# One-core recurrent attention with two MLP layers: keys of weight pieces renamed in a planned instruction order, one x split listed earlier, due times set anew

## The chip, the cores and the metric

The kernel runs on one core of one Trainium2 chip. The metric is device time in microseconds (us) of one execution, as the median of several runs. The engines are TensorE (PE in the profile; PEld is its load of the stationary operand), VectorE (DVE), ScalarE (ACT), GpSimd (POOL) and SyncE (SP, which issues the DMA transfers of this kernel). Each engine works through its own list of instructions in order.

## The reference

```python
def _attn_ref(r, k, v, w, u):          # B, H, S, D = 4, 8, 768, 48
    state = zeros(B, H, D, D)
    for t in range(S):
        cur = einsum('bhd,bhe->bhde', u[None] * k_t, v_t)
        y[:, :, t] = einsum('bhd,bhde->bhe', r_t, state + cur)
        state = w_t[:, :, :, None] * state + einsum('bhd,bhe->bhde', k_t, v_t)
x = attention output as 3072 tokens of 384
h = maximum(maximum(x @ w1, x @ w2), x @ w3)   # 384 -> 768
x = h @ w_out                                  # 768 -> 384
h = x @ w_in                                   # 384 -> 1024
solu = h * softmax(h)
out = (layernorm(solu) * g_ln) @ w_out         # 1024 -> 384
```

All of it is float32. The weights arrive as 64-bit words.

## The kernel before

**Units.** The sequence is cut into chunks of 128 tokens: 6 chunks of 4 batches give 24 units, numbered chunk by chunk, so that units 0 to 3 are the first chunk of the four batches and unit u takes the state that unit u - 4 left. `attend(u)` lists the steps of one unit: SP loads w, k, r (the feature-major parts, `load_part`), rk (token-major r and k) and v. DVE runs two scans over w, `s_sfx` (sf, L399, with pts L404 and a reciprocal) and `s_pfx` (pf, L416), scales r (rp, L420), multiplies rk by u and reduces it (rku, L433 and L439), and masks the scores (L481). POOL scales k (kt, L402), multiplies r by k (L429) and builds the diagonal (L449). TensorE computes the scores (sc, L474), up to unit 4 transposes k (kTp, L651), and then y in two parts: intra (L536) and, behind the state matmuls ds (L582), inter (L548). DVE ends the state (sbd, L610); from unit 5 on DVE also transposes k (kq, L632) for a trip through DRAM. ACT copies y out as xf (L662) and SP gathers rows of it (L668).

**Tiles.** Units form the tiles of the MLP: tile 0 is units 0 and 1, tile 1 is units 2 and 3, tile 2 is units 4 and 5; the later six tiles have three units each. `split(u)` turns x of unit u into a high part xh (ACT, L688) and a low part xl (POOL, L687), since each product is made of three matmuls. `layer_a(j)` lists 18 groups a{j}_{f}_{m} of nine matmuls (L737), six f by three m (w1, w2, w3). The first of the three results is copied by ACT (L742), the other two are folded in by DVE with max (L744); ACT and POOL then split h (L747, L750). `layer_b(j)` is the second matrix (L767). The groups a and b, the transposes and the conversion of weights share four PSUM banks.

**Weights.** The first layer's weights come in 24 pieces. `convert` lists for each: a load by SP (L1036), three ACT instructions (L311 to L313), a pair on DVE (L318, L323), then the high part (ACT, L332) and the low part (POOL, L336). Piece i, for i below 18, is what group i = 3f + m of a layer reads. Four raw buffers serve the loads, seven from piece 13 on, which lie over buffers of units 1 to 3.

**The order.** Nothing here is ordered by hand. `P.add` (L110 on) gives the planner a task: engine, estimated time, due time, and keys that it reads and writes. Dependencies come from the keys in the order in which tasks are listed: a reader depends on the last writer of the key, a writer on the last writer and all readers since. `order` then fills the engines in its own estimated time, and of the tasks that can start takes the one due first. Only the resulting lists reach the chip; there the engines wait for real buffers and results alone, not for the planner's keys. So a dependency between two things that merely share a key is a constraint on the order, and not a wait on the chip.

```python
r_, k_, w_ = ("r", u % 2), ("k", u if u < 3 else (u - 3) % 2), ("w", u if u < 3 else (u - 3) % 2)
add("SP", 400, -9000, lambda: load_part(u, 2), writes=[w_], kb=260)
done = convert(conv, "c", "w", C_DUE[0], C_DUE[1], 1.0, 384, banks=True, ...)
[(x_, k) for k in range(n)] + [("w", i)]
```

The first two lines are the keys of a unit's buffers in `attend`, with ("w", 0) to ("w", 2) for w; the third gives the converted pieces the keys ("w", 0) to ("w", 23); the fourth is what a group of `layer_a` reads. `due_of(u)` derives a unit's due times from `START`; `C_DUE` is the due time of the first piece and the step between pieces; `START[0]` and `START[1]` are those of layer a of tiles 0 and 1.

Of the kernel before, what the change touches and what calls it, by code (L numbers as in the profile page):

```python
# [23 lines left out]
KF1 = FF1 // 128  # L24
# [13 lines left out]
POST = (0, 1, 2, 2)  # L38
C3 = (4, 9, 1, 1, 1)
GAIN = 1  # L40
START = (34000, 48000, 100000, 7000)
BOTH, STEP, AHEAD = 41000, 45600, 20000
C_DUE = (14000, 3000)
SLACK = 1500
CUT = 0.5
GRP = [(0, 0), (0, 0), (0, 0), (1, 1), (1, 1, 1, 2)]
# [131 lines left out]
def emit(tc, general, flag, fm, tm, ub, wa, win, wo2, g, cst, half_cst, lmask, out):  # L178
# [9 lines left out]
    with ExitStack() as top:  # L188
# [481 lines left out]
        def s_xt(u):  # L670
            if u not in xf:
                return
            j = tile_of[u]
            n = tiles[j] * L
            if j not in xt:
                if j == 1:
                    o = 2 * KF1 * n
                    xt[j] = tuple(flat(wi)[:, o + i * KX * n:o + (i + 1) * KX * n].rearrange("p (a b) -> p a b", a=KX)
                                  for i in range(2))
                else:  # L680
                    if general or "x" not in xt:
                        xt["x"] = [xpool.tile([128, KX, n_max], F32R, tag=f"x{a}", name=f"x{a}{j}") for a in "hl"]
                    xt[j] = [t[:, :, 0:n] for t in xt["x"]]
            o = (u - first[j]) * L
            xh, xl = xt[j]
            x = xf.pop(u)
            low = lambda: G.tensor_tensor(xl[:, :, o:o + L], x[:, 0:KX], xh[:, :, o:o + L].bitcast(F32), op=ALU.subtract)  # L687
            A.activation(xh[:, :, o:o + L], x[:, 0:KX], AF.Copy)  # L688
            if general:
                low()  # L690
            else:
                at[u]["xl"] = low
# [109 lines left out]
        def second_weights():  # L802

            if not general:
# [22 lines left out]
        conv = Conv([sl(2 * (N_TMP + i), 2) for i in range(N_RAW)], [[sl(2 * t + i) for i in range(2)] for t in range(N_TMP)], jobs,  # L827
                    [stage[:, SPARE + 2 * i * CW:SPARE + 2 * (i + 1) * CW] for i in range(3)], SWITCH)
# [138 lines left out]
        def fast_phase1():  # L967
            P = Plan({"m": 4, "s": 1, "y": 1})
            n_unit = lambda j: range(first[j], first[j] + tiles[j])
            need = [START[0], START[1], START[2]]  # L970
            for j in range(3, n_tile):
                need.append(need[-1] + (BOTH if j == 3 else STEP))

            def due_of(u):
                j = tile_of[u]
                last = need[j] - AHEAD
                gap = (need[j] - need[j - 1]) / tiles[j] if j > 1 else START[3]
                return last - gap * (first[j] + tiles[j] - 1 - u)
# [47 lines left out]
            def split(u, after=()):  # L1026
                x_, o_ = ("xf", u % 3), (("x1" if tile_of[u] == 1 else "x"), u - first[tile_of[u]])
                P.add("ACT", 510, due_of(u) + 13000, lambda: s_xt(u), [x_], [o_], after)
                P.add("POOL", 1100, due_of(u) + 14000, lambda: at[u]["xl"](), [], [x_, o_])

            def convert(c, name, out, due, step, size, kb, after=(), extra=None, banks=False):
                lows = []
                for i in range(len(c.jobs)):
                    raw, tmp = (name, "raw", c.slot[i]), (name, "tmp", i % len(c.tmps))
                    t = due + step * i
                    P.add("SP", 400, t - 9000, lambda i=i: nc.sync.dma_start(c.raws[i], c.jobs[i][0]), [],  # L1036
                          [raw] + (extra(i) if extra else []), after, kb=kb)
                    key = ("m", (name, i)) if banks else None
                    bank = lambda: ps_m.tile([128, CW], F32, tag="m", name="cv") if banks else None
                    P.add("ACT", 1700 * size, t - 4000, lambda i=i: c.stage0(i, bank()), [raw], [tmp], take=key)  # L1040
                    P.add("DVE", 1150 * size, t - 2500, lambda i=i: (c.stage1(i), c.stage2(i)), [raw], [tmp], give=key,
                          port=0 if banks else 700)
                    P.add("ACT", 520 * size, t - 1200, lambda i=i: c.high(i), [tmp], [(out, i)])
                    P.add("POOL", 1100 * size, t - 1000, lambda i=i: c.low(i), [], [tmp, (out, i)])
                    lows.append(P.tasks[-1])
                return lows
# [3 lines left out]
            def layer_a(j, due, step, after=()):  # L1050
                n = tiles[j]
                sa, sb_, cur = moe[j] = moe_groups(j)
                x_, h_ = ("x1", "h1") if j == 1 else ("x", "h")
                for f in range(KF1):
                    for m in range(3):
                        key = ("a", j, f, m)
                        t_ = ("t", j, f % KX if j > 1 else 0)
                        i = 3 * f + m
                        g_ = P.add("PE", 9 * (174 if n == 3 else 120), due + step * i, lambda f=f, m=m: sa(f, m),
                                   [(x_, k) for k in range(n)] + [("w", i)], [("order", j)], take=("m", key))  # L1060
                        P.add("DVE" if m else "ACT", 560 if n == 3 else 430, 0, lambda f=f, m=m: cur["up", f, m](),
                              [], [t_], [g_, *after], give=("m", key))
                    P.add("ACT", 540 if n == 3 else 430, 0, lambda f=f: cur["hh", f](), [t_], [(h_, f)])
                    P.add("POOL", 1080 if n == 3 else 850, 0, lambda f=f: cur["hl", f](), [], [t_, (h_, f)])

            def layer_b(j, due, step, after=()):
                n = tiles[j]
                sa, sb_, cur = moe[j]
                h_ = "h1" if j == 1 else "h"
                w = 174 if n == 3 else 120  # L1070
                out = []
                for f0, f1 in ((0, KF1 - 1), (KF1 - 1, KF1)):
                    for m in range(KX):
                        key = ("b", j, m)
                        g_ = P.add("PE", 3 * (f1 - f0) * w, due + step * len(out), lambda m=m, f0=f0, f1=f1: sb_(m, f0, f1),
                                   [(h_, f) for f in range(f0, f1)] + [("w", 3 * KF1 + f) for f in range(f0, f1)] + [("order", j)],
                                   [("b", m)],
                                   take=("m", key) if f0 == 0 else None)
                        out.append(g_)
                for m in range(KX):  # L1080
                    P.add("ACT", 500 if n == 3 else 380, 0, lambda m=m: cur["x2", m](), [("b", m)], [], after,
                          give=("m", ("b", j, m)))
                return out
# [2 lines left out]
            P.add("SP", 400, 6000, lambda: nc.sync.dma_start(ident, cst[:, 128:]), [], ["ident"], kb=64)  # L1086
            P.add("SP", 400, 5000, lambda: nc.sync.dma_start(cs, half_cst), [], ["cs"], kb=64)
            for u in range(B):
                attend(u)
            over_spare = [[("k", 2), ("w", 2)], [("k", 2), ("w", 2), ("a", True)], [("a", True), ("rk", 2)]]  # L1090
            done = convert(conv, "c", "w", C_DUE[0], C_DUE[1], 1.0, 384, banks=True,
                           extra=lambda i: over_spare[conv.slot[i] - N_RAW] if conv.slot[i] >= N_RAW else [])
            for u in n_unit(0):
                split(u)
            layer_a(0, START[0], 2200, after=[])
            for u in n_unit(1):
                split(u)
            layer_a(1, START[1], 2200)
            for u in n_unit(2):
                attend(u)  # L1100
            for u in n_unit(2):
                split(u)
            b0 = layer_b(0, need[2] - 3000, 1500, done)
            b1 = layer_b(1, need[2] + 5000, 1500, done)
            for j in range(2, n_tile - 1):
                for u in n_unit(j + 1):
                    attend(u)
                t0 = need[j] + (15000 if j == 2 else 10000)
                if j == 3:
                    conv2 = middle_weights(6)  # L1110
                    c2 = convert(conv2, "c2", "w2", need[3] + 12000, (need[6] - need[3]) / len(conv2.jobs), 0.7, 192,
                                 after=[*done, *b0, *b1],
                                 extra=lambda i: ["ident", ("t", 0, 0), ("t", 1, 0)])
                layer_a(j, t0, (need[j + 1] - t0) / (3 * KF1), done + (c2 if j >= 6 else []))
                for u in n_unit(j + 1):
                    split(u)
                if j < n_tile - 2:
                    layer_b(j, need[j + 1], 1500, done + (c2 if j >= 6 else []))
# [243 lines left out]
```

## Time and profile before

| | |
|---|---|
| median of 3 runs | 655.57 us (654.66 to 658.0) |
| profiled execution, its own time | 655.7 us |
| its span in the trace | 653.9 us |
| mean granted clock of TensorE | 0.964 of 2.4 GHz |
| busy: PE, DVE, ACT, POOL | 92%, 66%, 45%, 59% of the span |
| DMA moved | 91.92 MB, mean 141 GB/s |

The profile is one execution. Its busy shares are means over very different stretches: the opening (attention of units 0 to 3 while the weights are loaded and converted), a middle in which groups a and b and attention alternate, and the second MLP from about 400 us on. "Idle before, releaser" names what ended the idle time in front of an instruction. A group's name carries no buffer numbers, so unit 3's and unit 4's instructions are told apart by their order.

### The profile page before, as it was taken

The page shows a single profiled execution, that of the slowest core. Times are in us where ns is not written, and L with a number is a line of the kernel's source. Part 1 is how long each engine was busy: PE and PEld are TensorE (multiplying, and loading weights), DVE is VectorE, ACT ScalarE, POOL GpSimd, SP SyncE. Part 2 cuts the span into 40 slices and gives each one's busy share as a digit, 9 for nine tenths or more (in the row PEclk, how much of TensorE's full clock was granted, in tenths as well). Part 3 has the DMA queues.
Part 4 walks back from the last instruction along what each step waited for, and adds up shares of the span by engine and source line. Part 5 has one row for each costly group of instructions (what it writes and reads, how often), then busy time and mean ns, then how long its engine had stood idle before and what let it go on. Part 6 is the DMA issues. An engine that isn't in the chain of part 4 may idle for free.

```text
span 653.9 us, 15400 instructions
## 1 busy us (share of the span) xinstructions
PE 598.9 (92%) x5926; PEld 555.7 (85%) x5926; DVE 429.6 (66%) x785; ACT 297.1 (45%) x689; POOL 384.1 (59%) x525
## 2 busy tenths in 40 slices
PE   3445889999999999999999989989999999999996
PEld 2345789999998999899999989988888888888995
DVE  7985888689999655654753233437777777777750
ACT  4688652346454223123222224644655555555551
POOL 4776666459768445445434212663877777777762
PEclk9666989999999999999999999999999999999999
DMA  9877234776664553643533102213666666666661
GB/s 319 318 236 269 94 101 92 206 210 162 201 187 121 152 140 78 193 120 98 145 87 86 20 4 82 82 37 71 155 152 154 153 153 153 154 153 153 145 130 55
DMA packets 174339, 91.92 MB, mean 141 GB/s; under 512 B 140976, under 2 KB 148912, under 8 KB 174256
## 3 DMA queue, kind: packets, MB, share of 16 engines
q1 hardware_dynamic: 174256, 90.84, 51.3%
q8 instruction: 49, 0.80, 0.5%
q14 instruction: 34, 0.28, 0.1%
HBM read 67.87 MB, written 21.76 MB: 137 GB/s over the span
## 4 chain that ended last, share of the span: by engine, by line
PE 73%; DVE 5%; DMA 3%; POOL 2%; issue 2%; ACT 1%; SPq 1%; DVEq 0%; ACTq 0%; POOLq 0%
PE a L737 27%; PE o L1251 15%; PE h L1174 14%; PE b L767 9%; PE y L548 3%; PE y L536 2%; PE sc L474 2%; PE ds L582 1%; DMA fk<-in_fm_dram 1%; DMA ct<-in_wo_dram 1%; DVE x L744 1%; DVE x L318 1%; DVE sf L399 1%; POOL h L750 1%; DMA kd<-sf 0%
## 5 line engine op out<-in xcount | busy, mean ns | idle before, releaser
L737 PE MATMUL a<-xh,wah 128*128 128x384 f32 (+1 forms) x432 | 144.6, 335 | 8.0 <-ACT xh L688 8.0
L737 PE MATMUL a<-xl,wah 128*128 128x384 f32 (+1 forms) x432 | 140.1, 324 | 2.2 <-POOL xl L687 2.2
L737 PE MATMUL a<-xh,wal 128*128 128x384 f32 (+1 forms) x432 | 139.9, 324 | 0.0
L1251 PE MATMUL o<-wo,lh 128*128 128x384 f32 x368 | 93.9, 337 | 0.0
L737 PEld LDWEIGHTS a<-xh,wah 128*128 128x128 f32 x432 | 82.6, 191 | 11.0 <-ACT xh L688 8.2
L1174 PE MATMUL h<-wi,x2h 128*128 128x512 f32 x288 | 91.8, 400 | 0.0
L750 POOL TENSOR_TENSOR h<-x,h 128x384 fp32r<-128x384 f32 (+1 forms) x48 | 53.5, 1114 | 61.0 <-ACT h L747 60.7
L744 DVE TENSOR_TENSOR x<-a,x 128x384 f32<-128x384 f32 (+1 forms) x108 | 54.2, 504 | 53.4 <-PE a L737 43.7
L737 PEld LDWEIGHTS a<-xl,wah 128*128 128x128 f32 x432 | 82.6, 191 | 2.5 <-POOL xl L687 2.5
L737 PEld LDWEIGHTS a<-xh,wal 128*128 128x128 f32 x432 | 82.6, 191 | 0.0
L1243 POOL TENSOR_TENSOR ll<-c,lh 128x512 fp32r<-128x512 f32 x44 | 64.6, 1490 | 21.7 <-ACT lh L1242 21.6
L767 PE MATMUL b<-h,wbh 128*128 128x384 f32 (+1 forms) x288 | 69.8, 328 | 0.0
L1251 PEld LDWEIGHTS o<-wo,lh 128*128 128x128 f32 x368 | 66.8, 188 | 1.8
L1174 PEld LDWEIGHTS h<-wi,x2h 128*128 128x128 f32 x288 | 54.4, 190 | 11.2
L1251 PE MATMUL o<-wo,ll 128*128 128x384 f32 x184 | 62.0, 337 | 0.0
L1174 PE MATMUL h<-wi,x2l 128*128 128x512 f32 x144 | 57.7, 401 | 2.9 <-POOL x2l L798 2.9
L1190 ACT ACTIVATE e<-h,sm 128x512 f32<-128x512 f32 x48 | 32.6, 684 | 57.9 <-DVE sm L1185 57.9
L747 ACT ACTIVATE h<-x 128x384 fp32r<-128x384 f32 (+1 forms) x48 | 23.7, 494 | 66.6 <-DVE x L744 53.0
L429 POOL TENSOR_TENSOR rk<-rk 128x384 f32<-128x384 f32 x23 | 26.4, 1150 | 44.8 <-DMA rk<-in_tm_dram 39.4
L767 PEld LDWEIGHTS b<-h,wbh 128*128 128x128 f32 x288 | 49.4, 189 | 1.4
L767 PE MATMUL b<-h,wbl 128*128 128x384 f32 (+1 forms) x144 | 46.3, 321 | 0.0
L1191 DVE SCALAR_TENSOR_TENSOR p<-h,e 128x512 f32<-128x512 f32 x48 | 32.7, 692 | 20.3 <-ACT e L1190 20.3
(139 smaller groups left out, 1233.6 us busy)
## 6 DMA issues: line engine op xcount, KB each, us to landing
pd<-q SPq DMA_DIRECT2D x23, 512.0 KB, 3.2
c<-pd SPq DMA_DIRECT2D x92, 128.0 KB, 3.8
x<-in_wa_dram SPq DMA_DIRECT2D x24, 384.0 KB, 4.9
rk<-in_tm_dram SPq DMA_DIRECT2D x23, 384.0 KB, 4.6
fr<-in_fm_dram SPq DMA_DIRECT2D x24, 256.0 KB, 4.4
v<-in_tm_dram SPq DMA_DIRECT2D x24, 256.0 KB, 3.5
fk<-in_fm_dram SPq DMA_DIRECT2D x23, 260.0 KB, 3.3
fk<-in_fm_dram SPq DMA_DIRECT2D x23, 256.0 KB, 2.9
```

What stands on the lines that cost most here:

```text
L429: G.tensor_tensor(t[:, 0:DM], t[:, 0:DM], t[:, DM:], op=ALU.mult)
L548: PE.matmul(d["yp"][o, j, p], s[o, p], rt[o, p, j * HL:(j + 1) * HL], start=False, stop=(p == NP - 1))
L737: PE.matmul(ps, w_[:, f, m, k], x_[:, k], start=(i == 0), stop=(i == 8))
L744: V.tensor_tensor(t, ps, t, op=ALU.max)
L747: A.activation(hh[:, f], t, AF.Copy)
L750: G.tensor_tensor(hl[:, f], t, hh[:, f].bitcast(F32), op=ALU.subtract)
L767: PE.matmul(ps, w_[:, f, m * 128:(m + 1) * 128], h_[:, f], start=(f == 0 and i == 0), stop=(f == KF1 - 1 and i == 2))
L1174: PE.matmul(ps, x_[:, k], w_[:, k, b * 512:(b + 1) * 512], start=(n_ == 0), stop=(n_ == 8))
L1190: A.activation(e[:, sl], d["h"][b], AF.Exp, bias=col(0), accum_out=col(2 + b))
L1191: V.scalar_tensor_tensor(p[:, sl], d["h"][b], 1.0, e[:, sl], op0=ALU.mult, op1=ALU.mult, accum_out=col(4 + b))
L1243: G.tensor_tensor(ll[:, b], c[:, b], lh[:, b].bitcast(F32), op=ALU.subtract)
L1251: PE.matmul(ps, l_[:, k], w_[:, k], start=(n_ == 0), stop=(n_ == 3 * KF2 - 1))
```

## The change

It renames the keys of the converted pieces from "w" to "wt" (for the second layer's weights from "w2" to "wt2"), where they are written and in both layers where they are read. It lists the split of unit 0 ahead of the attention of unit 3, which writes the same key of xf: in the loop over units 0 to 3 `split(u - 3)` is called in front of `attend(u)` from u = 3 on. `split(1)` stays behind the conversion, where before both stood. It sets the first layer's due time from 34000 to 24000 and the pieces' from 14000 with a step of 3000 to 20000 with a step of 2200 (the planner's nanoseconds). No instruction is added, removed or resized.

```diff
-START = (34000, 48000, 100000, 7000)
+START = (24000, 48000, 100000, 7000)
 BOTH, STEP, AHEAD = 41000, 45600, 20000
-C_DUE = (14000, 3000)
+C_DUE = (20000, 2200)
...
-                                   [(x_, k) for k in range(n)] + [("w", i)], [("order", j)], take=("m", key))
+                                   [(x_, k) for k in range(n)] + [("wt", i)], [("order", j)], take=("m", key))
...
-                                   [(h_, f) for f in range(f0, f1)] + [("w", 3 * KF1 + f) for f in range(f0, f1)] + [("order", j)],
+                                   [(h_, f) for f in range(f0, f1)] + [("wt", 3 * KF1 + f) for f in range(f0, f1)] + [("order", j)],
...
             for u in range(B):
+                if u >= 3:
+                    split(u - 3)
                 attend(u)
             over_spare = [[("k", 2), ("w", 2)], [("k", 2), ("w", 2), ("a", True)], [("a", True), ("rk", 2)]]
-            done = convert(conv, "c", "w", C_DUE[0], C_DUE[1], 1.0, 384, banks=True,
+            done = convert(conv, "c", "wt", C_DUE[0], C_DUE[1], 1.0, 384, banks=True,
                            extra=lambda i: over_spare[conv.slot[i] - N_RAW] if conv.slot[i] >= N_RAW else [])
-            for u in n_unit(0):
-                split(u)
+            split(1)
             layer_a(0, START[0], 2200, after=[])
...
-                    c2 = convert(conv2, "c2", "w2", need[3] + 12000, (need[6] - need[3]) / len(conv2.jobs), 0.7, 192,
+                    c2 = convert(conv2, "c2", "wt2", need[3] + 12000, (need[6] - need[3]) / len(conv2.jobs), 0.7, 192,
```

**TensorE, the end of unit 2, and unit 3.** Here y2 and y3 are the outputs of units 2 and 3 (the row with v is intra, the one with st is inter), sc3 the scores of unit 3, a0_f_m the groups of tile 0. Before:

```order
L651 MATMUL kTp3_480<-x2_66,fk0_96 128x128 x4
L548 MATMUL y2_435<-fr2_95,st1_2_487 64x64 x8
L474 MATMUL sc3_513<-fr0_93,fk0_96 64x64 x16
L536 MATMUL y3_550<-x2_66,v3_363 64x64 x16
L582 MATMUL ds3_574<-v3_363,kT3_508 64x64 x16
L548 MATMUL y3_550<-fr0_93,st1_3_604 64x64 x8
L737 MATMUL a0_0_0_684<-xh0_476,wah_110 128x256
```

Now, with the first matmul of each group alone:

```order
L651 MATMUL kTp3_482<-x2_66,fk0_96 128x128 x4
L737 MATMUL a0_0_0_502<-xh0_375,wah_110 128x256
...
L737 MATMUL a0_0_2_548<-xh0_375,wah_110 128x256
...
L548 MATMUL y2_438<-fr2_95,st1_2_490 64x64 x8
L737 MATMUL a0_1_0_578<-xh0_375,wah_110 128x256
...
L474 MATMUL sc3_606<-fr0_93,fk0_96 64x64 x16
...
L536 MATMUL y3_670<-x2_66,v3_369 64x64 x16
L582 MATMUL ds3_694<-v3_369,kT3_517 64x64 x16
...
L548 MATMUL y3_670<-fr0_93,st1_3_742 64x64 x8
```

Before, all of unit 3 stands ahead of the first group; now three groups stand ahead of y2's inter part, one more ahead of sc3, two ahead of y3 and two ahead of its inter part.

**DVE, around the scan of unit 4.** sf4 is that scan, s3 the end of unit 3's rku, cv a pair's first half, x2 scratch. Before:

```order
L744 TENSOR_TENSOR x2_66<-a0_2_2_840,x2_66 128x256
L318 SCALAR_TENSOR_TENSOR cv_851<-cv_851,x2_66 128x384
L323 SCALAR_TENSOR_TENSOR x2_66<-x2_66,cv_851 128x384
L744 TENSOR_TENSOR x2_66<-a1_0_2_857,x2_66 128x256
L398 MEMSET d1_103 128x4
L399 SCALAR_TENSOR_TENSOR sf4_885<-fk1_97,d1_103 128x520
```

Now:

```order
L610 TENSOR_TENSOR sbd2_108<-ds2_459,st1_2_490 128x256
L433 TENSOR_TENSOR rk3_293<-rk3_293,u_sb_98 128x384
L439 TENSOR_REDUCE s3_515<-rk3_293 128x8
L318 SCALAR_TENSOR_TENSOR cv_494<-cv_494,x2_66 128x384
L323 SCALAR_TENSOR_TENSOR x2_66<-x2_66,cv_494 128x384
L398 MEMSET d1_103 128x4
L399 SCALAR_TENSOR_TENSOR sf4_538<-fk1_97,d1_103 128x520
L404 TENSOR_SCALAR pts_99<-sf4_538 128x4
L405 RECIPROCAL d1_103<-pts_99 128x4
L744 TENSOR_TENSOR x2_66<-a0_0_1_520,x2_66 128x256
```

The scan of unit 4 stood behind the max of group a1_0_2 and stands now behind unit 3's rku and one pair; the first max of tile 0 follows it.

## Rows read from the trace of the kernel before

**Rows 1.** The page's busy time, share of the span and instructions of TensorE.

```profile
PE 598.9 (92%) x5926; PEld 555.7 (85%) x5926; DVE 429.6 (66%) x785; ACT 297.1 (45%) x689; POOL 384.1 (59%) x525
```

**Rows 2.** Busy us by stretch: start:end, length, each engine's, clock, DMA share, GB/s.

```profile
10.00:50.00 40.00, 18.63 (x432) 15.53 (x432) 36.92 (x59) 30.49 (x68) 29.14 (x26) 0.67 0.86 298
37.84:111.30 73.46, 53.97 (x677) 51.23 (x678) 56.45 (x102) 46.52 (x108) 51.64 (x50) 0.84 0.51 165
40.00:60.00 20.00, 6.63 (x95) 5.99 (x96) 13.74 (x23) 15.81 (x36) 14.22 (x16) 0.51 0.98 345
108.60:200.00 91.40, 91.27 (x1391) 86.52 (x1391) 78.13 (x134) 44.20 (x121) 60.20 (x58) 1.00 0.68 186
```

**Rows 3.** The chain that ended last, up to 110 us: start us, us, what.

```profile
93.90 14.72 PE a L737 x126
108.62 0.62 PE y L536 x32
```

**Rows 4.** TensorE's timeline: start us, us, operation, count, [idle before, releaser].

```profile
26.74 1.12 PE L548 MATMUL y<-fr,st 64*64 64x64 f32 x16 [1.38 <-ACT st L606]
...
38.31 0.69 PE L474 MATMUL sc<-fr,fk 64*64 64x64 f32 x32 [1.01 <-DVE sbd L610]
41.17 1.13 PE L536 MATMUL y<-x,v 64*64 64x64 f32 x32 [2.17 <-ACT cv L312]
...
45.16 1.12 PE L548 MATMUL y<-fr,st 64*64 64x64 f32 x16 [2.00 <-ACT st L606]
54.25 0.58 PE L737 MATMUL a<-xh,wah 128*128 128x256 f32 x1 [7.97 <-ACT xh L688]
...
57.44 0.41 PE L737 MATMUL a<-xh,wal 128*128 128x256 f32 x1
57.65 0.41 PE L737 MATMUL a<-xh,wah 128*128 128x256 f32 x1
```

**Rows 5.** POOL's timeline, 32 to 37 us.

```profile
32.95 1.17 POOL L402 TENSOR_TENSOR fk<-fk,sf 128x512 f32<-128x512 f32 x1
35.30 1.00 POOL L687 TENSOR_TENSOR xl<-xf,xh 128x384 fp32r<-128x384 f32 x1 [1.18 <-ACT xh L688]
```

**Rows 6.** DVE's timeline.

```profile
33.21 2.00 DVE L416 TENSOR_TENSOR_SCAN pf<-fk,d 128x520 f32<-128x520 f32 x1
...
37.84 0.41 DVE L610 TENSOR_TENSOR sbd<-ds,st 128x256 f32<-128x256 f32 x1
...
73.23 1.24 DVE L399 TENSOR_TENSOR_SCAN sf<-fk,d 128x520 f32<-128x520 f32 x1
...
111.26 0.70 DVE L632 STREAM_TRANSPOSE sf<-fk 128x512 f32<-128x512 f32 x1
...
112.64 0.55 DVE L433 TENSOR_TENSOR rk<-rk,u_sb 128x384 f32<-128x384 f32 x1
113.30 0.55 DVE L439 TENSOR_REDUCE s<-rk 128x8 f32<-128x384 f32 x1
...
117.72 0.17 DVE L404 TENSOR_SCALAR pts<-sf 128x4 f32<-128x4 f32 x1
...
136.03 1.23 DVE L416 TENSOR_TENSOR_SCAN pf<-fk,d 128x520 f32<-128x520 f32 x1
```

**Rows 7.** SP's timeline: the issue of transfers.

```profile
64.56 0.91 SPq L224 DMA_DIRECT2D fk<-in_fm_dram  x2
```

**Rows 8.** Groups by line and shape, 0 to 110 us: count, busy us, mean ns, idle before.

```profile
L311 ACT ACTIVATE x<-x,bias 128x384 f32<-128x384 uint32 x24 | 15.3, 639 | 10.3 <-DMA x<-in_wa_dram 10.2
...
L318 DVE SCALAR_TENSOR_TENSOR cv<-cv,x 128x384 int32<-128x384 int32 x24 | 13.4, 557 | 4.7 <-ACT x L313 4.6
...
L416 DVE TENSOR_TENSOR_SCAN pf<-fk,d 128x520 f32<-128x520 f32 x7 | 12.0, 1711 | 0.1
...
L433 DVE TENSOR_TENSOR rk<-rk,u_sb 128x384 f32<-128x384 f32 x7 | 5.5, 784 | 1.3 <-POOL rk L429 1.3
L404 DVE TENSOR_SCALAR pts<-sf 128x4 f32<-128x4 f32 x8 | 5.3, 658 | 0.3
```

## The prediction, made before the change was run

> **What bounds the kernel now.** I read the page's busy line, the busy table by stretch, the chain that ended last, TensorE's timeline of the opening and the rows of those that work beside it. TensorE is busy 598.9 of 653.9 us, so all it can win is 55 us [rows 1]. From 93.90 us on the chain runs through TensorE without a break, and from 108.60 to 200 us it works 91.27 of 91.40 us at a granted clock of 1.00, the level of 2.4 GHz; from 40 to 60 us it works 6.63 of 20 at 0.51, nearly all of it at 1.2 GHz [rows 2, 3]. At 108.62 us the last a1 group is done and y5, the next attention step, starts [rows 3]. From there on both kernels give TensorE nearly the same list, so I treat what follows as a block that moves with this point, and forecast when the point comes.
>
> In front of it the reader is to see TensorE without work that it might do [rows 4]: the last matmuls of unit 3 (y3 inter) start at 45.16 us, the first a0 group at 54.25, after 7.97 us of waiting for ACT's xh, which is unit 0's x. Unit 1's x, one unit later, was split long before, at 36.30 us [rows 5]. So it is the order that is short of work, not an engine. DVE had none either: its share is 92.3% from 10 to 50 us (36.92 of 40), but 69% from 40 to 60 (13.74 of 20) [rows 2], since unit 4's scan sf4 starts only at 73.23 us [rows 6]. SP issued two w transfers at 64.56 us, directly behind the first a0 groups [rows 7]: the planner took the keys of w buffers 0 and 1 and of weights 0 and 1 for the same thing.
>
> **The change, part by part.** *Splits and the start of a0.* No instruction is added or taken away. Eight a0 groups now stand between kTp3 and y3 inter and 12 in front of the first a1 group, where there were none and seven. A group is nine matmuls: at the half clock they follow each other every 0.21 us (57.44 to 57.65 [rows 4]), 1.9 us a group; in the chain 126 matmuls take 14.72 us, 1.05 us a group [rows 3].
>
> *False dependencies.* sf4 stands behind unit 3's rku on DVE, instead of behind a max of a1_0: DVE has work through the hole.
>
> *Due times.* Pieces of weights start later and follow more closely. On DVE the work ahead of sbd2 (the end of unit 2's state, at 37.84 us [rows 6]) is the same by count: one conversion pair more (2 x 0.56 us), one rku with its reduction less (2 x 0.55) [rows 6, 8]. SP brings unit 1's k, w and r ahead of u and cs; rku0, which needs u, now stands behind sf1 on DVE, so the later u has other work in front of it. I keep 37.84 us for sbd2.
>
> *The sum* goes by DVE. From 37.84 to 111.30 us, just behind the last max of a1 (kq7 follows it at 111.26), DVE is busy 56.45 us [rows 2, 6]; the new list also puts kq7, rku8 and its reduction ahead of that max, 0.70 + 0.55 + 0.55 [rows 6]: 58.25 us. At the share that DVE held where it did have work, 92.3%, they take 63.1 us and end at 100.9 instead of 111.3: **10.4 us**. Bounds: with no idle time at all they end at 96.1, 15.2 us earlier; at the share of that old stretch itself (56.45 of 73.46, 77%) they end at 113.6, 2.3 us later. I take 92.3% because the stretch from 10 to 50 has the same mixture of scans, pairs and masks, with the DMA engines at 0.86.
>
> From this goes what denser packing costs. The scan pf takes 1.23 us alone and 2.00 us where POOL's kt works beside it (32.95 to 34.12) [rows 5, 6]. Over 110 us the inflated kinds cost 7 x (1.71 - 1.23) for pf, 7 x (0.78 - 0.55) for rku and 8 x (0.66 - 0.17) for pts [rows 6, 8]: 8.9 us, half of it in my stretch. POOL's 51.64 us there are 70% of the time now and would be 82% of 63.1 us [rows 2]; 4.4 us grow by a sixth, 0.7, or 0.8 at DVE's share. **9.6 us are left**, and DVE's end is at 101.7.
> The Trainium skill (SBUF — State Buffer, "two separate sides") says that a DVE instruction with two SBUF inputs and a GpSimd instruction shut each other out for a whole instruction. An estimate by it: 17 such DVE instructions, each waiting half of a POOL instruction of 1.1 us in 82 of 100 cases, cost 7.7 us where I have 5.1, and the gain is 6.8 us, the time 648.8. By that rule, the trace agrees for pf: 34.12 + 1.23 is 35.35, and it ended at 35.21.
>
> *TensorE must be there too.* y3 inter ran at 45.16; eight groups at the half clock (15.2 us) go in front of it, less the 1.01 + 2.17 + 2.00 us in which TensorE stood there [rows 4]: 55.2. From y1 inter (26.74) to the end of unit 1's split (36.30) it was 9.6 us [rows 4, 5]; so unit 3's x is ready at 64.8, and a1 can start, with 24 groups left (25.2 us at full clock) and an estimated 3.2 us of attention between them, five steps of 0.5 to 0.9 us like y5's 0.62 [rows 3]. TensorE could be done at 93.2. By DVE's sum it is done at 99.0, as far ahead of the last max as now (108.6 to 111.3). DVE decides, by 5.8 us.
>
> *What hides the rest.* Behind the point TensorE is busy throughout and DVE 78.13 of 91.40 us [rows 2]; both lists move together, so I expect nothing to be given back. SP: the w transfers of units 4 and on go out earlier, the volume is the same, and the DMA engines' share from 37.84 to 111.30 is 0.51 [rows 2]. That costs nothing as long as each piece is there before its pair; if not, the first rival holds.
>
> The profiled execution took 655.7 us (span 653.9); less 9.6 it is 646.1. The median of the three runs shown, 655.57, is 0.13 lower: **646.0 us**.
>
> **The rivals.** *Weights come late.* A piece's buffer comes free with an earlier pair, SP issues in order, ACT needs three instructions, then DVE: the loads run at DVE's own pace. Over 24 pieces ACT stood 10.2 us for them, 0.43 each, of which 4.6 reached DVE [rows 8]. If all of that reached DVE for the 17 pieces left, it is 7.2 us: gain 2.4, **653.2 us**. For it: ACT's list is as full there as DVE's. Against: the DMA engines have room after 60 us. 12%.
> *The half clock stays.* Place: a0 and a1 groups with attention between them, where the granted clock was 0.51 with TensorE a third busy [rows 2]. Price: 0.85 us a group. Were all 24 groups left at 64.8 us and the attention beside them at 1.2 GHz, they would take 45.6 + 6.4 us, to 116.8 instead of 108.6: **663.8 us, slower**. It costs something from 25% of that work on (93.2 reaches 99.0), and makes the kernel slower by over 0.5% from 79% on (111.9). Against: the mean clock of the old stretch is 0.84 although it has 40 to 60 us in it [rows 2]. 4%.
> The Trainium skill (TensorE: Matmul & The Clock Gate, "The HAM clock gate") says that the throttled level is the default and that activity lifts it, so gaps between groups would cost clock. By that rule, no run shows yet whether these gaps do.
> *a0 waits for unit 1's x, and all behind it.* a0_0_0 now stands ahead of y2 inter and sc3 on TensorE, its first max ahead of mask3 and sbd3 on DVE. DVE reaches that max 4.9 us behind 37.84 (sbd2, rku3, a pair, sf4) and two groups at the half clock need 3.8, so x ready at 38.9 costs nothing (36.30 before). Each later us costs one: the gain is gone at 48.5, from 51.8 on it is slower by over 0.5%; at 52, 659.1 us. For it: unit 1's rows stand behind one more piece on SP. 5%.
> *DVE without idle time:* the bound above, **640.4 us**; 10% for under 643.
>
> **How the numbers follow.** Forecast 69% (643 to 652.3), full DVE 10%, late weights 12%, half clock 4%, x of unit 1 5%. 0.5%, 3.3 us, is about what a measurement of this kernel can tell from no change. Faster 0.79, same 0.12, slower 0.09. The range goes from the bound without idle time, 640.4, to late weights, 653.5; outside are the two slow rivals, part of the late weights and a little at the low end: two in ten.
>
> **What would show it.** Right: the first a0 group near 35 us instead of 54, sf4 near 41 instead of 73, the last a1 group done near 99, DVE's share from 38 us to there near 92%, and TensorE unbroken behind it as now. Wrong: DVE idle before its pairs, for ACT, by over 7 us in total; a granted clock near 0.5 beyond 65 us; a0_0_0 waiting for xl beyond 39 us; or TensorE standing between 110 and 200 us, which would mean that the block doesn't simply move.

## The result, and the profile after

The changed kernel took 645.52 us (median of 4 runs, 644.86 to 646.87) beside 656.53 us for the kernel before (654.66 to 658.0) on the same chip: a ratio of 0.9836, with a 95% interval of 0.9804 to 0.9869. The forecast was 646.0. The profiled execution took 645.44 us and spans 643.6, against 653.9 before.

The page's busy line of the changed kernel, to set beside [rows 1]:

```profile
PE 600.4 (93%) x5926; PEld 556.6 (86%) x5926; DVE 429.3 (67%) x785; ACT 295.7 (46%) x689; POOL 382.3 (59%) x525
```

The work is the same to 0.3% on every engine but ACT and POOL (0.5%); what went is idle time. Where it went is seen in the busy table by stretch (start:end, length, then PE, PEld, DVE, ACT, POOL busy, granted clock, DMA share, GB/s), to set beside [rows 2] (the clock figures of the first and third row are taken up in the last section):

```profile
10.00:50.00 40.00, 25.58 (x432) 22.27 (x435) 37.48 (x61) 29.71 (x68) 31.81 (x26) 1.00 0.82 288
38.59:103.23 64.64, 54.80 (x689) 50.35 (x688) 57.75 (x105) 45.56 (x107) 50.03 (x47) 0.95 0.60 188
40.00:60.00 20.00, 14.36 (x201) 12.37 (x201) 19.02 (x36) 16.15 (x37) 17.68 (x17) 0.97 0.78 268
108.60:200.00 91.40, 91.40 (x1324) 86.39 (x1323) 77.23 (x129) 43.55 (x123) 61.07 (x59) 1.00 0.62 178
```

From 40 to 60 us TensorE works 14.36 us where it worked 6.63, DVE 19.02 where it worked 13.74. The second row is the stretch of the prediction's sum, from unit 2's sbd2 to the end of the last a1 max: DVE is busy 57.75 us in 64.64; before it was 56.45 in 73.46. So DVE's idle time there fell from 17.0 to 6.9 us.

DVE's timeline (start us, us, line, operation, count, [idle before, releaser]); it answers to [rows 6]:

```profile
38.59 0.41 DVE L610 TENSOR_TENSOR sbd<-ds,st 128x256 f32<-128x256 f32 x1
...
41.77 1.24 DVE L399 TENSOR_TENSOR_SCAN sf<-fk,d 128x520 f32<-128x520 f32 x1
...
43.35 0.41 DVE L744 TENSOR_TENSOR x<-a,x 128x256 f32<-128x256 f32 x1
...
88.42 0.42 DVE L744 TENSOR_TENSOR x<-a,x 128x256 f32<-128x256 f32 x1 [0.15 <-PE a L737]
92.67 1.01 DVE L420 TENSOR_TENSOR fr<-fr,pf 128x512 f32<-128x512 f32 x1 [3.83 <-DMA fr<-in_fm_dram]
...
102.28 0.95 DVE L744 TENSOR_TENSOR x<-a,x 128x256 f32<-128x256 f32 x2 [0.39 <-ACT x L742]
```

Unit 4's scan starts at 41.77 us (73.23 before), the first a0 max at 43.35, and the last a1 max ends at 103.23. The one long hole left stands in front of 92.67 us: DVE's rp6 waits 3.83 us for unit 6's r. SP's timeline shows that this transfer was issued only at 86.70 us, behind v6 and rk9:

```profile
85.56 0.62 SPq L253 DMA_DIRECT2D v<-in_tm_dram  x1
86.29 0.36 SPq L248 DMA_DIRECT2D rk<-in_tm_dram  x1
86.70 0.43 SPq L224 DMA_DIRECT2D fr<-in_fm_dram  x1
```

The chain that ended last (start us, us, what) runs through it, where in the kernel before it ran through TensorE alone from 93.90 us on [rows 3]:

```profile
86.70 5.94 DMA fr<-in_fm_dram
...
99.71 1.30 PE a L737 x9
```

TensorE's timeline of the opening, to set beside [rows 4]:

```profile
36.28 0.56 PE L737 MATMUL a<-xh,wah 128*128 128x256 f32 x1
37.21 0.58 PE L737 MATMUL a<-xl,wah 128*128 128x256 f32 x1 [0.37 <-POOL xl L687]
...
40.58 0.41 PE L737 MATMUL a<-xl,wah 128*128 128x256 f32 x1
40.79 0.41 PE L737 MATMUL a<-xh,wal 128*128 128x256 f32 x1
...
42.41 0.28 PE L737 MATMUL a<-xh,wal 128*128 128x256 f32 x1
42.53 0.28 PE L737 MATMUL a<-xh,wah 128*128 128x256 f32 x1
...
54.94 0.68 PE L548 MATMUL y<-fr,st 64*64 64x64 f32 x16 [1.19 <-ACT st L606]
...
59.14 0.58 PE L737 MATMUL a<-xh,wah 128*128 128x256 f32 x1 [2.16 <-DVE x L744]
...
68.34 0.47 PE L737 MATMUL a<-wi,wah 128*128 128x256 f32 x2 [1.48 <-DVE x L323]
...
101.57 0.50 PE L767 MATMUL b<-h,wbh 128*128 128x256 f32 x2
```

The first a0 group starts at 36.28 us (54.25 before), y3 inter runs at 54.94, and the first group of the second matrix (b) at 101.57, against 109.66 us in the kernel before: 8.1 us earlier.

### The profile page after: what moved, and what is told of

Same layout as the page of the kernel before. It is cut to its first block, busy times and chain, and to the rows that moved or that the text cites. A ratio compares the mean times of both kernels' runs of the same rounds, so it can differ in the third digit from the quotient of the medians.

```text
span 643.6 us, 15413 instructions
## 1 busy us (share of the span) xinstructions
PE 600.4 (93%) x5926; PEld 556.6 (86%) x5926; DVE 429.3 (67%) x785; ACT 295.7 (46%) x689; POOL 382.3 (59%) x525
## 4 chain that ended last, share of the span: by engine, by line
PE 73%; DVE 5%; DMA 3%; issue 2%; POOL 2%; ACT 2%; SPq 0%; DVEq 0%; ACTq 0%; POOLq 0%
PE a L737 26%; PE o L1252 16%; PE h L1175 14%; PE b L767 10%; PE y L548 3%; PE sc L474 2%; PE y L536 2%; PE ds L582 1%; DMA fr<-in_fm_dram 1%; DVE x L744 1%; POOL h L750 1%; POOL wo L336 1%; DMA kd<-sf 1%; DVE x L318 1%; DVE sf L399 1%
## 5 line engine op out<-in xcount | busy, mean ns | idle before, releaser
L750 POOL TENSOR_TENSOR h<-x,h 128x384 fp32r<-128x384 f32 (+1 forms) x48 | 51.1, 1065 | 62.3 <-ACT h L747 62.2
L747 ACT ACTIVATE h<-x 128x384 fp32r<-128x384 f32 (+1 forms) x48 | 23.7, 493 | 67.5 <-DVE x L744 54.3
L429 POOL TENSOR_TENSOR rk<-rk 128x384 f32<-128x384 f32 x23 | 25.1, 1093 | 31.7 <-DMA rk<-in_tm_dram 29.8
```

The lines of the kernel that those rows point to most:

```text
L429: G.tensor_tensor(t[:, 0:DM], t[:, 0:DM], t[:, DM:], op=ALU.mult)
L747: A.activation(hh[:, f], t, AF.Copy)
L750: G.tensor_tensor(hl[:, f], t, hh[:, f].bitcast(F32), op=ALU.subtract)
```

## The experiments

**Theory A**, from the prediction: up to the last a1 max DVE is the bound, and the time follows how full DVE is there. **Rival B:** TensorE's early start with a0 brings the gain. **Rival C:** the weights' new due times bring it. **Rival D:** DVE's waits are only an effect of something as late as they are.

Each figure in the table is from that kernel's own profiled execution; the ratio is to the kernel before on the same chip, with its 95% interval. "DVE busy + idle" is for the stretch from sbd2 to the end of the last a1 max; "PE idle" is 110 us less TensorE's busy time from 0 to 110. A profiled execution is one of several: that of "due" was the slowest of its ten (664.92 us, the median 660.11), that of "split" the fastest of its ten (654.84, the median 658.43), so small differences between rows say little.

| kernel | ratio | first a0 | sf4 | DVE busy + idle | first b | PE idle |
|---|---|---|---|---|---|---|
| before | 1 | 54.3 | 73.2 | 56.5 + 17.0 | 109.7 | 41.4 |
| keys | 0.9895 [0.9854, 0.9935] | 53.5 | 44.3 | 59.9 + 5.9 | 103.8 | 34.3 |
| split | 1.0026 [1.0000, 1.0052] | 39.7 | 67.8 | 56.0 + 17.5 | 110.6 | 40.5 |
| due | 1.0051 [1.0025, 1.0076] | 52.6 | 67.3 | 54.8 + 20.7 | 112.6 | 42.6 |
| keys, split | 0.9868 [0.9837, 0.9899] | 42.5 | 45.3 | 60.9 + 3.4 | 102.2 | 31.7 |
| keys, due | 0.9976 [0.9949, 1.0004] | 54.9 | 40.8 | 60.8 + 9.8 | 109.9 | 37.4 |
| split, due | 1.0031 [1.0010, 1.0051] | 38.0 | 81.0 | 55.7 + 18.3 | 109.5 | 42.4 |
| all (changed) | 0.9836 [0.9804, 0.9869] | 36.3 | 41.8 | 57.8 + 6.9 | 101.6 | 31.2 |
| three r keys | 0.9866 [0.9838, 0.9895] | 37.8 | 42.7 | 57.1 + 8.4 | 103.0 | 35.7 |
| r6 first | 0.9803 [0.9770, 0.9835] | 36.2 | 41.7 | 57.9 + 5.5 | 99.9 | 28.2 |

**One part alone.** The keys:

```diff
-[(x_, k) for k in range(n)] + [("w", i)]
+[(x_, k) for k in range(n)] + [("wt", i)]
...
-done = convert(conv, "c", "w", ...
+done = convert(conv, "c", "wt", ...
```

> The kernel before with the renaming of the weights' keys alone (splits and due times as before). In its order sf4 stands right behind unit 2's sbd2 and pairs, but the first a0 group comes behind all of unit 3's matmuls and sc4. Theory A (DVE's share between 38 us and the last a1 max sets the time, and any work that fills it is as good as other): most of the gain is here, 646 to 650 us, sf4 near 43 us, DVE share from 38 us to the last a1 max at least 88%. Rival B (TensorE's early start with a0 brings it): a0 starts not before 54 us as in before, and the time is 653 to 658 us.

Measured: 648.7 us, sf4 at 44.26, DVE 91% busy, the first a0 group at 53.53. Of the two theories A holds: a0 starts as late as before, and two thirds of the gain are there.

The split:

```diff
             for u in range(B):
+                if u >= 3:
+                    split(u - 3)
                 attend(u)
...
-            for u in n_unit(0):
-                split(u)
+            split(1)
```

> The kernel before with the split of the first units' x moved alone (keys and due times as before). In its order a0_0_0 stands ahead of y3, near 42 us, but sf4 stays behind a max of a0 and the pairs. Theory A: DVE still runs out of work between 42 and 65 us since sf4 is late; 651 to 656 us, sf4 behind 60 us. Rival B (the early a0 brings the gain): 645 to 650 us.

Measured: 658.43 us, above the range of A and far from B's: a0 starts 14.5 us earlier and nothing is won. DVE's waits from 40 to 110 us (engine and line, what it waited for, us in total, times, longest) show a DVE whose list holds little but pairs and maxes whose inputs are not there yet:

```profile
DVE cv L318 <- ACT x L313: 6.9, 4, 2.8
DVE x L744 <- PE a L737: 4.4, 2, 2.9
```

The due times:

```diff
-START = (34000, 48000, 100000, 7000)
+START = (24000, 48000, 100000, 7000)
-C_DUE = (14000, 3000)
+C_DUE = (20000, 2200)
```

> The kernel before with the due times alone (START 24000, C_DUE 20000 and 2200). In its order a0_0_0 is behind y3 inter and sf4 late, both as before. Theory A and rival B: within 2 us of before, 654 to 658 us, since neither false dependency nor split has changed. Rival C (the gain is that the pieces of weights come in another rhythm): 646 to 651 us.

Measured: 660.11 us, 0.5% slower than before, a little over what A allowed for and the opposite of C.

**Two parts together.** The changed kernel without its split:

> The changed kernel without the moved split (keys and due times alone). In its order the first a0 group stands behind sc4, as with the keys alone, and sf4 directly behind sbd2. Theory A: since DVE has attention and weights to do in that time, the late a0 costs little: 646 to 650 us, like the keys alone (648.7). Rival B (the early a0 is worth what the keys alone lack): 651 to 655 us.

Measured: 656.21 us, a miss for A and a little above B's range. DVE does have its work: it is busy 19.15 of 20 us from 40 to 60. What is late is TensorE. In the stretch from 100 to 110 us it works without a break, while DVE is half idle (start:end, length, then PE, PEld, DVE, ACT, POOL busy, granted clock):

```profile
40.00:60.00 20.00, 8.97 (x156) 7.62 (x149) 19.15 (x30) 14.90 (x34) 16.48 (x15) 1.00 0.91 286
100.00:110.00 10.00, 10.00 (x112) 9.81 (x111) 4.96 (x11) 2.63 (x7) 3.39 (x4) 1.00 0.19 74
```

DVE's waits from 40 to 110 us are now for TensorE's groups and for ACT's copies of them:

```profile
DVE x L744 <- ACT x L742: 3.4, 2, 1.7
DVE x L744 <- PE a L737: 2.7, 5, 0.7
```

So the theory was too narrow. **Theory F** in its place: two things must hold together, work for DVE between 38 and 65 us, and an a0 early enough that TensorE isn't the bound at the end. By F the keys alone just pass the second with the old due times; with the new ones the gain is gone. F was made to fit this run; its tests are the two runs below. Between this kernel and the keys alone the first b differs by 6.1 us (109.88 against 103.83). The stretches from the first a0 to the first b, here and then with the keys alone, hold the same 549 matmuls:

```profile
54.91:109.88 54.97, 49.26 (x549) 47.06 (x549) 45.65 (x84) 32.67 (x78) 39.62 (x38) 0.97 0.51 152
53.53:103.83 50.30, 46.94 (x549) 44.75 (x549) 45.31 (x84) 32.06 (x76) 40.15 (x38) 0.94 0.58 172
```

So 1.4 us is the later start of a0 (TensorE waits 3.4 us for xh against 0.5), 2.3 us is more idle time within the stretch (3.0 us for pairs of weights against 1.1, 2.1 for xl against 1.1), and 2.3 us is longer matmuls: they stand 0.21 us apart up to 62 us and again from 69 to 73, with the keys alone only up to 59. This last part is the rate of TensorE and not its place in the order; no run takes the two apart.

The changed kernel with the due times of before, and the one with the old keys:

> The changed kernel with the due times of before (keys and split alone). In its order a0_0_0 stands directly behind sc3 and sf4 directly behind mask3 and a pair, so that DVE has work from 38 us on and TensorE has a0 groups from about 42 us on. Theory F (two things must hold together: DVE has attention and weights to do between 38 and 65 us, and TensorE starts a0 early enough not to be the bound at the end): both hold, 645 to 650 us, a ratio to before of 0.982 to 0.990. Rival C (the due times are what brings the pieces in time): at most a third of the gain, 652 to 657 us.

Measured: 648.11 us, as F expected. The due times are worth 0.3% here by the two ratios, but the intervals of this kernel and the changed one overlap, so that this is not clear of noise; alone they cost 0.5%.

> The changed kernel with the old keys (split and due times alone). In its order two a0 groups stand ahead of sc3, but sf4 comes behind the second max of a1_0 and sc4 behind a0_5_0. Theory F: the first condition fails, DVE is idle for 12 us or more between 45 us and the last a1 max, and the time is no better than before's, 654 to 661 us, a ratio of 0.997 to 1.007. Rival B (the early a0 is what counts): 645 to 650 us.

Measured: 658.67 us, with 18.3 us of DVE idle, as F expected. 10.9 us of it is in front of pairs, for ACT, by DVE's waits from 40 to 110 us:

```profile
DVE cv L318 <- ACT x L313: 10.9, 9, 2.6
```

**More work on DVE.** In both kernels the reduction of s_diag is done four times for units 3 to 8:

```diff
-            V.tensor_reduce(s, h3(rk_t[u][:, 0:DM]), axis=AX.X, op=ALU.add)
+            for _ in range(4 if 3 <= u <= 8 and not general else 1):
+                V.tensor_reduce(s, h3(rk_t[u][:, 0:DM]), axis=AX.X, op=ALU.add)
```

> The changed kernel with the reduction of s_diag (0.55 us on DVE) done four times instead of once for units 3 to 8: 18 more of them, 9.95 us of DVE's time, all between sbd2 and the last a1 max; results and orders are unchanged. Theory A (DVE bounds): the work added goes onto the time but for what the waits for r take up (5.3 us at most): 5 to 10 us longer than the changed kernel, a ratio to before of 0.991 to 0.999. Rival D (DVE is not the bound): 0 to 3 us longer, 0.984 to 0.988.

> The kernel before with the same 18 reductions more. There DVE stood idle for some 17 us between 38 us and the last a1 max, much of it between 45 and 61 us. Theory A (in before the order leaves DVE short of work, so added work fills holes): 0 to 4 us longer, a ratio of 1.000 to 1.006, clearly less than the changed kernel loses by the same work. Rival E (DVE's work counts fully in both, the holes come elsewhere): 8 to 10 us longer, 1.012 to 1.016.

Measured: 650.8 us, a ratio of 0.9906 [0.9868, 0.9943], for the changed kernel; 660.11 us, 1.0051 [1.0023, 1.0078], for the kernel before. The busy table from sbd2 to the end of the last a1 max, first of the changed kernel with the added work:

```profile
38.21:110.96 72.75, 60.18 (x703) 56.25 (x702) 66.16 (x123) 45.18 (x107) 50.22 (x47) 0.88 0.56 170
```

and then of the kernel before with it:

```profile
39.35:114.15 74.80, 56.03 (x684) 52.62 (x685) 62.76 (x114) 45.49 (x105) 52.90 (x49) 0.98 0.51 156
```

In the changed kernel DVE is busy 8.4 us longer (66.16 against 57.75) and the stretch is 8.1 us longer: by these sums DVE's work counts there nearly in full. It is not DVE's work alone, though. The wait for r fell from 3.83 to 0.3 us, which alone would have taken up part of the work, and TensorE spent more time at the half clock, among others from 72.36 to 79.18 us. The busy table of that stretch, with the added work and then in the changed kernel without it:

```profile
72.36:79.18 6.82, 5.99 (x28) 6.02 (x29) 5.23 (x12) 3.24 (x8) 2.76 (x4) 0.50 0.41 136
72.36:79.18 6.82, 6.82 (x109) 6.49 (x111) 6.53 (x14) 5.78 (x15) 6.70 (x7) 1.00 0.43 132
```

How much of the 8.1 us comes through TensorE was not separated. In the kernel before, unit 3's stand ahead of sbd2 and unit 8's behind the last a1 max, so 12 of the 18 are in the stretch: DVE is busy 6.3 us longer there (62.76 against 56.45), and the stretch grows by 1.3; the holes took it up. On the whole time the changed kernel lost 4.6 us (0.9906 - 0.9836, of 657 us), just below the range of A and above that of D. In the profiled executions its first b came at 107.52 instead of 101.57 and its span was 6.8 us longer (650.4 against 643.6); the profiled execution with the added work was the slowest of its four (652.22 us, the median 650.8), so the 5.9 us at b and the 4.6 us of the ratios are not to be set against each other. The kernel before lost 3.3, of which 1.5 is sbd2 itself (39.35 instead of 37.84), which unit 3's reductions pushed back.

**The wait for r.** The planner's key for r takes two buffers where the program has three, so that unit 6's r is planned behind unit 4's last reader: one more false dependency. First the key was set right:

```diff
-                r_, k_, w_ = ("r", u % 2), ...
+                r_, k_, w_ = ("r", u % 3), ...
```

> The changed kernel with one more key set right: r has three buffers in the program and two in the planner's keys, so that unit 6's r is planned behind the last reader of unit 4's. With three keys r6 goes out much earlier. In the changed kernel DVE stood 3.8 and 1.5 us for r. Theory A: DVE is what bounds this stretch, its 5.3 us of waiting for r go to 0 to 1, and the time falls by 3 to 5 us, to 640.5 to 642.5 us. Rival D (DVE's waits are only moved, because the other order makes another wait, for weights or for TensorE, or TensorE is the bound as well): 644 to 647 us.

Measured: 647.71 us, a ratio of 0.9866 [0.9838, 0.9895]. DVE's waits for r are gone, and nothing is won: rival D, though the time lies a little above D's range too. The new key moved the order of every engine; sf7 now waits for a kd, maxes for TensorE, and TensorE's idle time up to 110 us is 35.7 us instead of 31.2. DVE's waits in that kernel, 8 to 110 us:

```profile
DVE sf L399 <- DMA kd<-sf: 2.7, 2, 2.5
DVE x L744 <- PE a L737: 1.9, 3, 0.8
```

Then one transfer alone was moved on SP, and no other engine's order:

```diff
-        return sorted(out, key=lambda t: (t.start, t.n))
+        r6, kd5 = self.mark["r", 6], self.mark["kd", 5]; r6.start, r6.n = kd5.start, kd5.n - 0.5; return sorted(out, key=lambda t: (t.start, t.n))
```

> The changed kernel with one transfer issued earlier on SP: unit 6's r stands directly ahead of unit 5's kd (near 70 us) and not behind v6 and rk9 (86.70 us); the order of all other engines is the changed kernel's. Its buffer is unit 3's, free since y3 inter at 54.94 us. Theory A (DVE bounds the stretch up to the last a1 max): the 3.83 us in which DVE stood for this transfer go, the last a1 max ends near 100 us instead of 103.23 and the time falls by 2.5 to 4 us against the changed kernel's ratio to before of 0.984, to a ratio of 0.978 to 0.980 (642 to 643.5 us). Rival D (TensorE, which was busy 8.04 of 10 us from 90 to 100 us, or the weights are as late): less than 1 us is won, a ratio of 0.982 to 0.986.

Measured: 644.15 us, a ratio of 0.9803, at A's upper edge (in us 0.65 above it) and below D's. It was run a second time beside the changed kernel:

> The changed kernel itself, beside the one with unit 6's r issued earlier, on one chip. Both theories: a ratio to before of 0.980 to 0.987.

> The changed kernel with unit 6's r issued directly ahead of unit 5's kd, a second time, on the same chip as the changed kernel. Theory F (idle time of TensorE up to 110 us is what the time follows; it was 31.2 us in the changed kernel and 28.2 in this one): 2 to 4 us faster than the changed kernel beside it. Rival: the difference of the two ratios, 0.9836 and 0.9803, was chance between chips, and it is within 1 us.

Measured: 645.61 us (644.34 to 647.41) for the changed kernel, 642.58 us (640.66 to 643.57) for this one, with ratios of 0.9820 [0.9784, 0.9856] and 0.9767 [0.9732, 0.9802]: 3.0 us faster, and no run of the one within the runs of the other. It beats both kernels. (F is put there as: the time follows TensorE's idle time up to 110 us. The column "PE idle" bears that out but for two rows out of order; as TensorE's busy time over the whole span is nearly the same in all, it tells where the loss is seen rather than what causes it.) SP's row in that second run:

```profile
67.13 0.38 SPq L224 DMA_DIRECT2D fr<-in_fm_dram  x1
```

DVE's waits there from 36 to 102 us:

```profile
DVE x L744 <- ACT x L742: 1.4, 2, 1.0
DVE sf L399 <- DMA kd<-sf: 0.3, 1, 0.3
```

The 3.83 us are gone; 1.0 of them came back, since the maxes wait 1.4 us for ACT's copies where they waited 0.4, and DVE's idle time in the stretch is 4.6 us (57.78 busy of 62.37).

## Why the prediction was right

**The sum.** The last a1 max was to end at 101.7 us and ended at 103.23. By the terms: sbd2 came 0.75 us later than kept (38.59), DVE's work was 57.75 us instead of 58.25, the 0.8 us for denser packing did not show in it, and DVE was idle 6.9 us instead of 4.85. That gives +0.75 - 0.5 - 0.8 + 2.04 = +1.5 us. The longest wait in those 6.9 us, 3.83, is one that the prediction left out: of SP it said that the earlier transfers cost nothing as long as each piece of the weights is there before its pair. They were (DVE's 4.6 us of waiting for ACT in front of pairs fell to 0, and ACT's for pieces from 10.2 to 7.3), but of r, which SP also brings, it said nothing. The groups of the changed kernel, 0 to 110 us, to set beside [rows 8]:

```profile
L311 ACT ACTIVATE x<-x,bias 128x384 f32<-128x384 uint32 x24 | 15.3, 638 | 7.3 <-DMA x<-in_wa_dram 7.3
L318 DVE SCALAR_TENSOR_TENSOR cv<-cv,x 128x384 int32<-128x384 int32 x24 | 13.3, 553 | 0.0
```

**Packing.** POOL's 50.03 us are 77% of the stretch; 82% was forecast. The groups of the same stretch (count, busy us, mean ns, idle before):

```profile
L416 DVE TENSOR_TENSOR_SCAN pf<-fk,d 128x520 f32<-128x520 f32 x4 | 6.7, 1682 | 0.0
L399 DVE TENSOR_TENSOR_SCAN sf<-fk,d 128x520 f32<-128x520 f32 x4 | 6.0, 1500 | 0.2
...
L404 DVE TENSOR_SCALAR pts<-sf 128x4 f32<-128x4 f32 x4 | 2.3, 579 | 0.1
```

The same groups of the kernel before, from 37.84 to 111.30 us:

```profile
L416 DVE TENSOR_TENSOR_SCAN pf<-fk,d 128x520 f32<-128x520 f32 x4 | 6.8, 1712 | 0.1
L399 DVE TENSOR_TENSOR_SCAN sf<-fk,d 128x520 f32<-128x520 f32 x4 | 5.0, 1250 | 0.2
L404 DVE TENSOR_SCALAR pts<-sf 128x4 f32<-128x4 f32 x4 | 2.6, 662 | 0.1
```

pf and pts are a little shorter than before, sf is 0.25 us longer each time: the inflation mostly changed its place, and these twelve instructions together grew by 0.6 us (15.0 against 14.4). All of DVE's records in the stretch add up to 62.5 us, 2.8 more than the 59.7 before, where the sum with its packing term has 2.5 to 2.6 more. But they cover only 57.75 us (56.45 before), because successive instructions overlap by 4.7 us instead of 3.2. So the packing term is of about the right size, and what the sum had no term for is the overlap. The Trainium skill (SBUF — State Buffer, "two separate sides") has the two engines shut each other out for a whole instruction; the estimate made from that, a gain of 6.8 us, was too low in this case, the last a1 max having come 8.1 us earlier.

**TensorE.** The last a1 group was to be done at 99.0 us and was at 101.01, 2.2 us ahead of the last max where 2.7 were forecast: it moved with DVE. That TensorE alone could have been done at 93.2, and that DVE decides by 5.8 us, no run shows. That DVE's work counts in the changed kernel the added reductions bear out, with the half clock mixed in; and it is a matter of the order: without the split TensorE decides.

**The half clock.** Eight groups in front of y3 inter were costed at 0.21 us a matmul. Two were: from 36.28 to 41 us matmuls follow each other every 0.21 us (40.58 to 40.79), and from 42 us on every 0.12 (42.41 to 42.53). Still y3 inter came at 54.94, as forecast (55.2). That is luck: six groups at the full clock saved some 5 us, and TensorE lost about as much, 3.8 us of idle time between 36.28 and 54.94 us (1.28 of it for a copy by ACT, 1.19 for ACT's st), which the sum had left out, and the 0.75 us by which sbd2 came later. The rival in which the half clock stays came true in a small part: behind TensorE's waits at 54.94 and 59.14 us, of 1.19 and 2.16 us, the granted clock was 0.50 from 59 to 65 us. DVE was busy 5.79 of these 6 us, and TensorE then waited 1.48 us for a pair, so little of it can have reached DVE; what it cost was not measured. The Trainium skill (TensorE: Matmul & The Clock Gate, "The HAM clock gate") has the throttled level come back after idleness; the trace agrees in that the clock fell at 58.79 us, within the wait of 2.16 us.

**The block behind.** It was to move as a whole. It moved by 8.1 us at the first b and by 10.3 at the end of the span. From 110 to 600 us TensorE was idle 5.7 us instead of 7.4: y's inter part waited 0.2 us for the states from DVE where it had waited 1.6. So in the profiled executions 1.5 us too much was forecast in front, and 2 us of gain behind was not forecast at all. On the medians the gain was 11.0 us (656.53 to 645.52) where 9.6 was forecast; the forecast counted from 655.57 us, 1.0 below the median measured here. That it is only 0.5 us off is therefore luck in part: these errors offset each other, while the mechanism, DVE's list filled and b 8 us earlier, is as forecast.

**The parts.** The prediction took splits, keys and due times in one sum. The runs tell their shares: the keys carry it (1.1% alone); the split wins nothing alone and 1.4% where keys and due times stand; the due times win about 0.3% with the other two, not clear of noise, and cost 0.5 to 0.8% without the split.

## What to carry to other kernels

Where an opening is bound by the order and not by an engine, sum the work of the fullest engine up to the point where the next engine runs without a break, and ask of each input of that engine, not only of those that the change names, when its transfer is issued. A false dependency in a planner costs through what it pushes back, so its parts interact: test them in pairs before giving one the credit. And a dependency set right in the planner moves everything; one transfer moved by hand tells what that transfer was worth.

## What was not expected of the hardware

The granted clock of the busy table and the spacing of matmuls seem to disagree in the opening. In the changed kernel the table reads a clock of 1.00 from 36 to 42 us, where the matmuls of the first two groups stand 0.21 us apart, the spacing that in the kernel before goes with 0.51 [rows 2, 4]; later the two agree (0.50 from 59 to 65 us):

```profile
36.00:42.00 6.00, 5.13 (x23) 4.54 (x23) 5.74 (x11) 5.39 (x15) 4.42 (x4) 1.00 0.77 243
59.00:65.00 6.00, 5.10 (x39) 4.59 (x42) 5.79 (x10) 5.89 (x14) 3.77 (x5) 0.50 0.69 197
```

The trace settles it. Its clock record has its first entry only at 41.72 us, a rise to the full clock, and the table counts what lies ahead of the first entry as full. From that entry on the two agree: the matmuls stand 0.12 us apart from 42 us on, and 0.21 from 58.8 to 65.6 us, where the record has 0.50. With keys and due times the first entry is at 62.6 us, the matmuls of a0 stand 0.21 us apart up to there, and the table reads 1.00 from 40 to 60 us. So ahead of the first entry the rate is to be read from the starts of the matmuls, and a mean clock over the span (0.991 here, 0.964 before, where the first entry is at 16.45 us) is no measure of what the change won there.

Nor does the time follow how long the half clock lasts: of the first layer's matmuls up to 112 us, 31 follow each other at 0.21 us in the kernel before and 23 with the keys alone, but 44 in the changed kernel and 50 with r6 first, the fastest.
